# Seven-product blocks issued in program order on four engines, and the weights' sums moved to GpSimd

## The chip, the cores and the metric

The kernel runs on one core of a Trainium2 chip. The engines named here are TensorE (PE; its weight loads are PEld), VectorE (DVE), ScalarE (ACT), GpSimd (POOL) and SyncE (SP), whose queue starts most of the DMA transfers. The metric is the device time of one launch in microseconds, lower is better.

## What is computed

Three layers follow each other on 4 x 768 = 3072 tokens: a retention attention with 8 heads of 64, a gated layer (512 to 1536 and back) behind an RMS norm, and a layer with softmax, layer norm and an output product (512 to 1024 to 512).

```python
state = gamma * state + einsum('bhd,bhe->bhde', k[t], v[t])
y[t]  = scale * einsum('bhd,bhde->bhe', q[t], state)        # attention, one token after the other
xn = x / sqrt(mean(x*x) + 1e-6) * rms_g
g, val = xn @ w_gate, xn @ w_val
x  = (g * sigmoid(g) * val) @ w_out                         # gated layer
h  = x @ w_in
solu = h * softmax(h)
out = (solu - mean) / sqrt(var + 1e-6) * g_ln @ w_out2      # last layer
```

## The kernel before, in words

The tokens run in six blocks of 512 (n = 0 to 5). A block has two parts. In the **gated part** 12 steps (m = 0 to 11) each make 128 columns of gate and 128 of value, and add their share of the output product into four PSUM banks X0 to X3. The **last part** (`de_block`, four tiles of 128 tokens) makes softmax, layer norm and the last product.

Every fp32 product is three fast products: operands are split into a high part (an ACT cast) and a low part (a subtraction), and `mm3` issues high x high, high x low, low x high as three matmuls; in the trace these are L583, L584 and L585 whatever the product.

Blocks 0 and 1 make gate and value with plain products (`bc_block`). Blocks 2 to 5 (`n >= FROM`) use a scheme with seven products for eight (`bc_block7`): a 2 x 2 block product from seven products of sums, `prod(1)` to `prod(7)`, each six matmuls of 256 columns into one of four quarters of the banks GB and VB in turn. So a product waits until the fourth one before it has been taken out of its quarter. One step takes them out so: ACT copies products 1 and 5 (tile `s15`), DVE adds on products 6 and 7 (`u23`), GpSimd adds `u23` and `s15` into `c` twice (L698, L700), and DVE adds products 2, 3 and 4 into `c`. Then ACT makes the Silu of the gate half (L707), DVE multiplies by the value half (L712), and `split` makes the high part (ACT, L89, the tile called r below) and the low part (DVE, L90). `cm(d)` (`cmm`) adds the step **before** into output bank d: three matmuls of 512 columns for each of the four banks.

The seven products need sums of the weights, split as well. The sums are made once, while the last parts of blocks 1 and 0 run one after the other: `s_fetch(m)` loads the weights' parts, `s_make(m)` adds high and low on DVE (L627) into `st` tiles, makes four more sums on GpSimd (L631 to L634) and stores them. In the blocks `s_load(g)` loads a pair of them into two of three `st` buffers, and `s_split(g)` casts both on ACT (L308) and subtracts both on GpSimd (L309).

The attention of block n+1 runs inside the gated part of block n: `att_pieces` gives 24 pieces, three for each of 8 units. Piece a makes scores (PE, an ACT copy, two DVE operations, L151 to L153); piece b makes the other scores, one output product and the next unit's preparation (two ACT casts, two DVE subtractions L117 and L119, two GpSimd products L126); piece c updates the state (GpSimd L191, DVE L194), makes the second output product, the next GpSimd product L135 and, for every second unit, takes out the output with a DVE reduction (L214). `slot(n, s)` calls what is due at slot s, three slots to a step; the 24 pieces fall two to a step. The norm of block n+1 (`rms_steps`) has slots in the last part.

The order of instructions on each engine is not the order in which they are written: when the kernel is built, a scheduler with a model of time arranges all that is ready. Each engine then runs its own row strictly in order, with semaphore waits between the rows.

Of the kernel before, what the change touches and what calls it, by code (L numbers as in the profile page):

```python
# [2 lines left out]

# [6 lines left out]
F32 = mybir.dt.float32  # L10
F32R = mybir.dt.float32r
# [4 lines left out]
ALU = mybir.AluOpType  # L16
AX = mybir.AxisListType

P = 128
# [3 lines left out]
NM = 12  # L23
# [13 lines left out]
FROM = 2  # L37
# [3 lines left out]
def retention_moe_kernel(ctx: ExitStack, tc: tile.TileContext, qk0, q2, kt, kv, wpk, w2i, w2o,  # L41
                         rg, gl, sel, mtab, qtab, ktab, utab, out):
    nc = tc.nc
# [26 lines left out]
    U0 = cp.tile([P, 3, 4, P], F32, tag="w2oh", name="U0")  # L70
    UF = [None, U0[:, 0], U0[:, 1], U0[:, 2], U[0]]

    cnt = [0]

    def wt(tag, shape, dt, bufs):
        cnt[0] += 1
        return wp.tile(shape, dt, tag=tag, name=f"{tag}_{cnt[0]}", bufs=bufs)

    def st():
        return wt("st", [P, 512], F32, 3)  # L80

    def f4():
        return wt("f4", [P, 2, 512], F32, 3)
# [221 lines left out]
    Lq, Hq = slice(0, 256), slice(256, 512)  # L305
# [250 lines left out]
    def at(s, f, *a):  # L556
        wsched.setdefault(s, []).append((f, a))

    def w_plan():
        for g in range(2, NG):  # L560
            for part in range(3):
                if g < NM:
                    s = 3 * (g - 2) + part
                    at(s, w_split, g, part)
                    at(s - 1, w_conv, g, part)
                    at(s - 3, w_load, g, part)
                else:
                    at(3 * g - 4 + part if part < 2 else 3 * g, w_load, g, part)
# [44 lines left out]
    sscr = [[dp.tile([P, 2, 256], F32, tag=f"s{m}_{i}", name=f"s{m}_{i}") for i in range(2)] for m in range(NM)]  # L613
    sums = {}

    def s_fetch(m):
        for part in range(2):
            w = wt("wo", [P, 2, 2, 256], F32R, 2)
            nc.sync.dma_start(w.bitcast(F32), scr[m][part])
            sums[m, part] = w  # L620

    def s_make(m):
        ts = []
        for part in range(2):
            hi, lo = parts(sums.pop((m, part)), part)
            t = st().rearrange("p (h x) -> p h x", h=2)
            nc.vector.tensor_tensor(out=t, in0=hi.bitcast(F32), in1=lo.bitcast(F32), op=ALU.add)  # L627
            ts.append(t)
        g, v = ts
        G = nc.gpsimd  # L630
        G.tensor_tensor(out=v[:, 1], in0=v[:, 0], in1=v[:, 1], op=ALU.add)  # L631
# [3 lines left out]
        for i in range(2):  # L635
            nc.sync.dma_start(sscr[m][i], ts[i])
# [31 lines left out]
    def bc_block7(n):  # L668

        base = 3 * NM * n  # L670
        V, G = nc.vector, nc.gpsimd
        for m in range(NM):
            g = n * NM + m
            c = f4()
            s15, u23 = (wt("r2", [P, 2, 256], F32, 8) for _ in range(2))

            def prod(i):
                q = quarter[0] % 4
                quarter[0] += 1
                ps = GV[q // 2][:, q % 2 * 256:q % 2 * 256 + 256]  # L680
                product(i, g, ps)
                return ps

            def cm(*ds):
                if m:
                    cmm(g - 1, m - 1, ds)

            def add(eng, out, x, y):
                eng.tensor_tensor(out=out, in0=x, in1=y, op=ALU.add)  # L689

            if m + 2 < NM:
                s_load(g + 2)
            nc.scalar.copy(s15[:, 0], prod(1))
            w_slot(base + 3 * m)
            add(V, u23[:, 0], prod(6), s15[:, 0])
            slot(n, 3 * m)
            nc.scalar.copy(s15[:, 1], prod(5))  # L697
            add(G, c[:, 0, Hq], u23[:, 0], s15[:, 1])  # L698
            add(V, u23[:, 1], prod(7), u23[:, 0])
            add(G, c[:, 1, Hq], u23[:, 1], s15[:, 1])  # L700
            cm(0)
            slot(n, 3 * m + 1)
            w_slot(base + 3 * m + 1)
            add(V, c[:, 0, Lq], prod(2), s15[:, 0])
            cm(1)
            add(V, c[:, 0, Hq], prod(3), c[:, 0, Hq])
            nc.scalar.activation(c[:, 0, :], c[:, 0, :], AF.Silu)  # L707
            if m == NM - 1 and n and PRE & 2:
                nc.scalar.activation(wt("sm", [P, 12], F32, 4)[:, 0:1], c[:, 0, 0:1], AF.Exp)
            cm(2)  # L710
            add(V, c[:, 1, Lq], prod(4), u23[:, 1])
            V.tensor_tensor(out=c[:, 1, :], in0=c[:, 1, :], in1=c[:, 0, :], op=ALU.mult)  # L712
            ah, al = r2(), r2()
            split(ah, al, c[:, 1, :])
            acts[m] = (ah, al)
            shl.pop(g)
            if m + 2 < NM:
                s_split(g + 2)
            slot(n, 3 * m + 2 if m < NM - 1 else 34)
            cm(3)  # L720
            w_slot(base + 3 * m + 2)
        cmm(n * NM + NM - 1, NM - 1)

    extra = {}
# [142 lines left out]
    def de_block(n, srcs, base):  # L867

        x2_split(srcs)
        slot(n, base)  # L870
        d_mm(n, 0, base + 1)
        d_mm(n, 1, base + 3)
        t_tr(0)
        d_mm(n, 2, base + 5)
        t_tr(1)
        e_mm(n, 0, base + 7)
        d_mm(n, 3, base + 9)
        t_tr(2)
        e_mm(n, 1, base + 11)
        t_tr(3)  # L880
        e_mm(n, 2, base + 13)
        e_mm(n, 3, base + 15)
# [123 lines left out]
    for n in range(NB):  # L1006
        if n + 1 < NB:
            if n == 0:
                span, r = 30, (31, 33, 34, 34, 35, 35)
            elif n == 1:  # L1010
                span, r = 45, (47, 49, 50, 51, 52, 53, 54, 55, 56, 57)
            else:
                span, r = 35, (37, 38, 39, 40, 41, 42, 43, 44, 45, 46)
            pieces = att_pieces(n + 1)
            for i, f in enumerate(pieces):
                extra.setdefault((n, i * span // (len(pieces) - 1)), []).append(f)
            for s, f in zip(r, rms_steps(SB, n + 1)):
                extra.setdefault((n, s), []).append(f)
        if n + 1 >= FROM and n + 1 < NB:
            for i in range(2):  # L1020
                s, g = (63 if n == 1 else 45) + 3 * i, (n + 1) * NM + i
                extra.setdefault((n, s), []).append(lambda g=g: s_load(g))
                extra.setdefault((n, s + 1), []).append(lambda g=g: s_split(g))
        if n == 1:
            for m in range(NM):
                extra.setdefault((n, 36 + 2 * m), []).append(lambda m=m: s_fetch(m))
                extra.setdefault((n, 37 + 2 * m), []).append(lambda m=m: s_make(m))
        (bc_block if n < FROM else bc_block7)(n)
        if n == 0:
            after.close()  # L1030
            x2_store()
            slot(0, 35)
            continue
        de_block(n, XB, 35)
        if n == 1:
            de_block(0, x2_load(), 52)

# [70 lines left out]
```

## Time and profile before

| | |
|---|---|
| median of 3 runs | 1217.53 us (1216.37 to 1218.59) |
| profiled execution | 1215.62 us, of this span 1213.8 us |
| PE busy | 1062.0 us, 87% of the span |
| DVE, ACT, POOL busy | 736.9, 500.7 and 607.8 us (61%, 41% and 50%) |
| mean granted TensorE clock | 0.960 of full speed |

The profile is one execution. A row of the time line gives the start, the time taken, the engine, the line, what is written from what is read, and in brackets the idle time before it and who ended it. A mean over the span mixes the six blocks, so the stretches are read one by one.

### The profile page before, as it was taken

How to read it: one execution, taken by the hardware profiler on the slowest of the kernel's cores; microseconds unless marked ns; L12 is line 12 of the kernel's file. 1: busy time of each engine (PE TensorE's matmuls, PEld its weight loads, DVE VectorE, ACT ScalarE, POOL GpSimd, SP SyncE). 2: the span in 40 equal slices, each digit the busy share in tenths (PEclk: the TensorE clock that was granted, in tenths of full speed). 3: DMA queues.
4: the chain of work that ended last, by engine and by line, in shares of the span. 5: the costliest groups of instructions: out<-in, count | busy, mean ns of one | idle time of the engine just before them, and what ended most of it. 6: DMA issues, size and time to landing. Idle time of an engine off the chain costs nothing.

```text
span 1213.8 us, 17407 instructions
## 1 busy us (share of the span) xinstructions
PE 1062.0 (87%) x6038; PEld 869.9 (72%) x6038; DVE 736.9 (61%) x1294; ACT 500.7 (41%) x985; POOL 607.8 (50%) x670
## 2 busy tenths in 40 slices
PE   8999999889988698878899878889978889888898
PEld 7777677567766587667688667767767768777777
DVE  6887779972758848753665764464754455334352
ACT  4556655542433454222454322346422245322233
POOL 6866748840567747534254644435444425334222
PEclk9899999989999799899999989989989989999999
DMA  9799888745675736455314555512435521355300
GB/s 335 229 315 348 291 307 288 284 157 187 224 234 183 228 111 210 157 174 182 113 48 146 173 160 179 175 51 83 153 125 195 169 102 53 122 182 183 122 1 35
DMA packets 81239, 212.77 MB, mean 175 GB/s; under 512 B 9472, under 2 KB 9856, under 8 KB 81152
## 3 DMA queue, kind: packets, MB, share of 16 engines
q1 hardware_dynamic: 72368, 186.49, 47.6%
q10 hardware_dynamic: 8784, 25.17, 5.2%
q8 instruction: 48, 0.79, 0.3%
q14 instruction: 39, 0.32, 0.1%
HBM read 179.12 MB, written 32.51 MB: 174 GB/s over the span
## 4 chain that ended last, share of the span: by engine, by line
PE 50%; DVE 17%; issue 8%; ACT 7%; DMA 4%; POOL 3%; DVEq 0%; SPq 0%; POOLq 0%; ACTq 0%
PE X L583 9%; PE X L584 8%; PE X L585 8%; PE GB L583 4%; DVE f L712 4%; PE GB L585 4%; PE GB L584 4%; PE VB L583 4%; PE VB L584 3%; PE VB L585 3%; DMA s<-st 2%; ACT r L89 2%; DVE st L488 2%; ACT x L308 2%; DVE xT L312 1%
## 5 line engine op out<-in xcount | busy, mean ns | idle before, releaser
L309 POOL TENSOR_TENSOR x<-st,x 128x512 fp32r<-128x512 f32 x96 | 133.0, 1404 | 66.2 <-ACT x L308 31.6
L689 POOL TENSOR_TENSOR f<-r,r 128x256 f32<-128x256 f32 x96 | 70.9, 758 | 185.8 <-ACT r L697 96.8
L583 PE MATMUL X<-r,wo 128*128 128x512 f32 x264 | 88.4, 442 | 64.6 <-ACT r L89 64.6
L584 PE MATMUL X<-r,wo 128*128 128x512 f32 x264 | 110.3, 418 | 4.1 <-DVE r L90 4.1
L585 PE MATMUL X<-r,wo 128*128 128x512 f32 x264 | 108.9, 413 | 0.0
L583 PEld LDWEIGHTS X<-r,wo 128*128 128x128 f32 x264 | 48.8, 202 | 81.0 <-ACT r L89 72.6
L308 ACT CAST x<-st 128x512 fp32r<-128x512 f32 x96 | 55.2, 619 | 105.9 <-issue 54.8
L487 POOL TENSOR_TENSOR st<-st,x 128x512 int32<-128x512 int32 x52 | 73.9, 1422 | 42.3 <-DVE st L486 21.9
L126 POOL TENSOR_TENSOR qd<-rq,qtab_t 64x256 f32<-64x256 f32 x68 | 63.9, 939 | 51.9 <-PE YB L163 44.8
L90 DVE TENSOR_TENSOR r<-f,r 128x512 fp32r<-128x512 f32 x72 | 65.9, 915 | 27.6 <-ACT r L89 27.4
L488 DVE SCALAR_TENSOR_TENSOR st<-st,sq 128x512 f32<-128x512 f32 x52 | 62.7, 1205 | 24.1 <-POOL st L487 23.1
L89 ACT CAST r<-f 128x512 fp32r<-128x512 f32 x72 | 44.5, 617 | 75.1 <-DVE f L712 57.5
L712 DVE TENSOR_TENSOR f<-f 128x512 f32<-128x512 f32 x48 | 52.1, 1085 | 21.9 <-ACT f L707 19.1
L584 PEld LDWEIGHTS X<-r,wo 128*128 128x128 f32 x264 | 53.3, 202 | 16.8 <-DVE r L90 6.4
L585 PE MATMUL X<-w2oh,r 128*128 128x512 f32 (+1 forms) x144 | 57.0, 396 | 4.4 <-DVE r L90 4.4
L583 PE MATMUL GB<-xnh,w 128*128 128x256 f32 (+1 forms) x172 | 59.2, 344 | 1.7 <-DVE r L689 1.7
L585 PEld LDWEIGHTS X<-r,wo 128*128 128x128 f32 x264 | 53.2, 202 | 10.5
L583 PE MATMUL VB<-xnh,w 128*128 128x256 f32 (+1 forms) x172 | 58.6, 340 | 0.0
L151 ACT COPY A<-SB 128x256 f32<-128x256 f32 x64 | 23.7, 371 | 83.4 <-PE SB L147 75.5
L583 PE MATMUL X<-w2oh,r 128*128 128x512 f32 (+1 forms) x144 | 57.7, 401 | 0.0
L585 PE MATMUL GB<-xnh,w 128*128 128x256 f32 (+1 forms) x172 | 57.0, 331 | 0.8 <-DVE w L90 0.8
L584 PE MATMUL GB<-xnl,w 128*128 128x256 f32 (+1 forms) x172 | 56.8, 330 | 0.6 <-DVE xnl L280 0.6
(297 smaller groups left out, 3333.2 us busy)
## 6 DMA issues: line engine op xcount, KB each, us to landing
wo<-scr SPq DMA_DIRECT2D x84, 512.0 KB, 3.4
w<-scr SPq DMA_DIRECT2D x72, 512.0 KB, 4.3
st<-s SPq DMA_DIRECT2D x96, 256.0 KB, 3.2
x<-in_wpk SPq DMA_DIRECT2D x36, 512.0 KB, 5.8
w<-scr SPq DMA_DIRECT2D x48, 256.0 KB, 3.3
rq<-in_q SPq DMA_DIRECT2D x40, 256.0 KB, 3.5
rv<-in_kv SPq DMA_DIRECT2D x40, 256.0 KB, 3.9
scr<-CV ACTq DMA_DIRECT2D x18, 512.0 KB, 4.7
```

The lines of the kernel that those rows point to most:

```text
L89: nc.scalar.copy(hi, src)
L90: (lo_eng or nc.vector).tensor_tensor(out=lo, in0=src, in1=hi.bitcast(F32), op=ALU.subtract)
L126: nc.gpsimd.tensor_tensor(out=qd[r], in0=tq4[r, :, hh, :], in1=qtab_t[r, 2 * u:2 * u + 2, :], op=ALU.mult)
L308: nc.scalar.copy(hi, src)
L309: eng.tensor_tensor(out=lo, in0=src, in1=hi.bitcast(F32), op=ALU.subtract)
L487: nc.gpsimd.tensor_tensor(out=ti, in0=ti, in1=lo, op=ALU.add)
L488: lastc[0] = nc.vector.scalar_tensor_tensor(out=t, in0=t, scalar=3.4028234663852886e38, in1=g, op0=ALU.min, op1=ALU.mult)
L583: nc.tensor.matmul(ps, lhsT=lh, rhs=rh, start=start, stop=False)
L584: nc.tensor.matmul(ps, lhsT=lh, rhs=rl, start=False, stop=False)
L585: nc.tensor.matmul(ps, lhsT=ll, rhs=rh, start=False, stop=stop)
L689: eng.tensor_tensor(out=out, in0=x, in1=y, op=ALU.add)
L712: V.tensor_tensor(out=c[:, 1, :], in0=c[:, 1, :], in1=c[:, 0, :], op=ALU.mult)
```

## The change

Around `bc_block7` a context `in_order` chains all instructions that the block issues on PE, DVE, ACT and POOL: each gets an edge, without a semaphore, to the one written before it on its engine. The rows of these four engines are then as written; SP's is not chained. The last instruction of each engine is kept in `tails`, and all of `de_block` is placed behind it. The body of the step is written in another order: `s_split` is for the next step and stands at the step's start, `cm(0)` and `cm(1)` follow products 2 and 3, and `cm(2, 3)` follows the split. `s_make` adds high and low on GpSimd in the load buffers, `s_fetch` runs two steps ahead with the buffers `w4` and `wo`, and the three first weight loads of block 2 (`late`) wait until the sums are done.

```diff
+    @contextmanager
+    def in_order():
+        cur = nc.cur_bb.bb.instructions
+        mark = cur[-1]
+        yield
...
+        for i in cur[start:]:
+            if i.engine in ORDERED:
+                if i.engine in last:
+                    tc.add_manual_dep(i, last[i.engine].name,
...
+                last[i.engine] = i
+        tails.clear()
+        tails.extend(last.values())
+    ORDERED = (E.PE, E.DVE, E.Activation, E.Pool)
...
     def s_fetch(m):
-        for part in range(2):
-            w = wt("wo", [P, 2, 2, 256], F32R, 2)
+        for part, (tag, bufs) in enumerate((("w4", 3), ("wo", 2))):
+            w = wt(tag, [P, 2, 2, 256], F32R, bufs)
...
     def s_make(m):
-            t = st().rearrange("p (h x) -> p h x", h=2)
-            nc.vector.tensor_tensor(out=t, in0=hi.bitcast(F32), in1=lo.bitcast(F32), op=ALU.add)
-            ts.append(t)
...
+        for hi, lo in (g, v):
+            G.tensor_tensor(out=hi.bitcast(F32), in0=hi.bitcast(F32), in1=lo.bitcast(F32), op=ALU.add)
...
+            nc.scalar.copy(s15[:, 0], prod(1))
+            add(V, u23[:, 0], prod(6), s15[:, 0])
+            if m + 1 < NM:
+                s_split(g + 1)
             if m + 2 < NM:
                 s_load(g + 2)
-            nc.scalar.copy(s15[:, 0], prod(1))
             w_slot(base + 3 * m)
-            add(V, u23[:, 0], prod(6), s15[:, 0])
             slot(n, 3 * m)
             nc.scalar.copy(s15[:, 1], prod(5))
             add(G, c[:, 0, Hq], u23[:, 0], s15[:, 1])
             add(V, u23[:, 1], prod(7), u23[:, 0])
             add(G, c[:, 1, Hq], u23[:, 1], s15[:, 1])
-            cm(0)
+            add(V, c[:, 0, Lq], prod(2), s15[:, 0])
             slot(n, 3 * m + 1)
             w_slot(base + 3 * m + 1)
-            add(V, c[:, 0, Lq], prod(2), s15[:, 0])
-            cm(1)
+            cm(0)
             add(V, c[:, 0, Hq], prod(3), c[:, 0, Hq])
             nc.scalar.activation(c[:, 0, :], c[:, 0, :], AF.Silu)
-            cm(2)
+            cm(1)
             add(V, c[:, 1, Lq], prod(4), u23[:, 1])
             V.tensor_tensor(out=c[:, 1, :], in0=c[:, 1, :], in1=c[:, 0, :], op=ALU.mult)
             split(ah, al, c[:, 1, :])
-            if m + 2 < NM:
-                s_split(g + 2)
             slot(n, 3 * m + 2 if m < NM - 1 else 34)
-            cm(3)
+            cm(2, 3)
             w_slot(base + 3 * m + 2)
...
-        (bc_block if n < FROM else bc_block7)(n)
+            with in_order():
+                bc_block7(n)
...
-        de_block(n, XB, 35)
+            for i in tails:
+                later.enter_context(tc.issue_after(i))
+            de_block(n, XB, 35)
```

On PE, in a step of block 5 before, the output product of a step (tile r, banks X_68 to X_71) stands as four high x high matmuls right behind the products (GB and VB are the banks of the quarters):

```order
L584 MATMUL VB<-xsl,x_1332_9257 128x256
L585 MATMUL VB<-xsh,x_1333_9258 128x256
L583 MATMUL X_68<-r_1342_9341,wo_9282 128x512
L583 MATMUL X_69<-r_1342_9341,wo_9282 128x512
L583 MATMUL X_70<-r_1342_9341,wo_9282 128x512
L583 MATMUL X_71<-r_1342_9341,wo_9282 128x512
L583 MATMUL GB<-xsh,x_1332_9257 128x256
```

After the change it stands, in the same block, bank by bank between products 2, 3 and 4:

```order
L612 MATMUL GB<-xnh,w_1368_9676 128x256
L610 MATMUL X_68<-r_1378_9754,wo_9705 128x512
L611 MATMUL X_68<-r_1379_9755,wo_9705 128x512
L612 MATMUL X_68<-r_1378_9754,wo_9705 128x512
L610 MATMUL GB<-xnh,x_1372_9695 128x256
```

So the output product now comes five products after the step that feeds it, and its first bank alone is behind product 2.

On ACT, the row of one step of block 5 before is: both copies (L693, L697), the two casts of the sums, the Silu and the cast of r:

```order
L693 COPY r_1396_9709<-GB 128x256
L697 COPY r_1396_9709<-VB 128x256
L308 CAST x_1404_9785<-st_9711 128x512
L308 CAST x_1404_9785<-st_9713 128x512
L707 ACTIVATE f_1395_9708<-f_1395_9708 128x512
L89 CAST r_1402_9781<-f_1395_9708 128x512
```

After the change the casts stand between the two copies:

```order
L716 COPY r_1394_9855<-VB 128x256
L329 CAST x_1396_9871<-st_9789 128x512
L329 CAST x_1396_9871<-st_9791 128x512
L724 COPY r_1394_9855<-GB 128x256
L733 ACTIVATE f_1393_9854<-f_1393_9854 128x512
L110 CAST r_1402_9930<-f_1393_9854 128x512
L716 COPY r_1406_9943<-VB 128x256
```

The first copy of the next step is now directly behind the cast of r in every step.

On GpSimd, a stretch of block 2 before has the attention (qd, kd, U), the sums' subtractions (x) and the two adds into c (tile f) in mixed order:

```order
L126 TENSOR_TENSOR qd_5044<-rq_4939,qtab_t 64x256 x2
L135 TENSOR_TENSOR kd_4937<-rv_4747,ktab_t 128x256
L191 TENSOR_TENSOR U_82<-U_81,utab_t 64x2x64 x2
L309 TENSOR_TENSOR x_616_4079<-st_3969,x_615_4078 128x512
L309 TENSOR_TENSOR x_616_4079<-st_3971,x_615_4078 128x512
L126 TENSOR_TENSOR qd_5621<-rq_5147,qtab_t 64x256 x2
L135 TENSOR_TENSOR kd_5145<-rv_4943,ktab_t 128x256
L191 TENSOR_TENSOR U_82<-U_81,utab_t 64x2x64 x2
L689 TENSOR_TENSOR f_618_4089<-r_620_4091,r_619_4090 128x256 x2
```

After the change a step with pieces b and c reads:

```order
L330 TENSOR_TENSOR x_630_4302<-st_4194,x_629_4301 128x512
L330 TENSOR_TENSOR x_630_4302<-st_4196,x_629_4301 128x512
L147 TENSOR_TENSOR qd_4330<-rq_4215,qtab_t 64x256 x2
L714 TENSOR_TENSOR f_626_4284<-r_628_4286,r_627_4285 128x256 x2
L212 TENSOR_TENSOR U_81<-U_82,utab_t 64x2x64 x2
L156 TENSOR_TENSOR kd_4371<-rv_4219,ktab_t 128x256
```

Both subtractions and the piece at the step's first slot now stand ahead of the adds into c; the attention is spread two pieces to a step over the whole block, where before it ran ahead.

## Rows read from the trace of the kernel before

**Rows 1.** Windows: PE, PEld, DVE, ACT, POOL busy (count), PEclk, DMA share, GB/s
```profile
446.20:597.87 151.67, 125.39 (x825) 106.52 (x824) 96.72 (x167) 58.56 (x121) 79.27 (x79) 0.94 0.54 171
648.50:799.04 150.54, 121.47 (x797) 103.47 (x795) 94.28 (x158) 55.50 (x114) 74.49 (x78) 0.93 0.52 168
850.00:990.43 140.43, 115.20 (x739) 99.90 (x739) 76.52 (x131) 48.81 (x99) 59.45 (x55) 0.95 0.48 156
1037.00:1161.95 124.95, 103.08 (x655) 91.37 (x655) 49.51 (x86) 36.10 (x73) 44.76 (x45) 0.99 0.45 146
597.87:648.50 50.63, 50.63 (x244) 40.74 (x244) 25.82 (x67) 22.96 (x48) 19.54 (x31) 1.00 0.20 61
307.30:446.20 138.90, 115.86 (x557) 90.89 (x556) 96.87 (x198) 55.71 (x117) 90.18 (x121) 0.91 0.63 199
```

**Rows 2.** Time line of PE: first of six, first of eight, the next product
```profile
744.18 0.28 PE L583 MATMUL GB<-xsh,x 128*128 128x256 f32 x1
...
744.88 0.39 PE L584 MATMUL X<-r,wo 128*128 128x512 f32 x1
...
746.71 0.28 PE L583 MATMUL VB<-xnh,x 128*128 128x256 f32 x1
```

**Rows 3.** Time line of PE in block 5: two output products, two steps apart
```profile
1078.14 1.21 PE L583 MATMUL X<-r,wo 128*128 128x512 f32 x4 [1.45 <-ACT r L89]
...
1098.36 1.19 PE L583 MATMUL X<-r,wo 128*128 128x512 f32 x4 [1.48 <-ACT r L89]
```

**Rows 4.** Groups by line and shape, ACT, 649 to 799 us: busy, mean ns, idle
```profile
L707 ACT ACTIVATE f<-f 128x512 f32<-128x512 f32 x12 | 7.5, 628 | 4.1 <-DVE f L689 4.1
L89 ACT CAST r<-f 128x512 fp32r<-128x512 f32 x12 | 7.4, 618 | 13.3 <-DVE f L712 13.3
L151 ACT COPY A<-SB 128x256 f32<-128x256 f32 x13 | 4.8, 370 | 22.3 <-PE SB L147 22.2
```

**Rows 5.** The same view for POOL, 649 to 799 us
```profile
L309 POOL TENSOR_TENSOR x<-st,x 128x512 fp32r<-128x512 f32 x20 | 27.7, 1400 | 9.3 <-PE GB L585 3.3 <-PE VB L585 3.3 <-ACT x L308 2.3
L689 POOL TENSOR_TENSOR f<-r,r 128x256 f32<-128x256 f32 x24 | 17.7, 756 | 37.5 <-ACT r L697 24.6 <-DVE r L689 12.8
L126 POOL TENSOR_TENSOR qd<-rq,qtab_t 64x256 f32<-64x256 f32 x10 | 9.2, 922 | 11.0 <-PE YB L163 10.6
L191 POOL TENSOR_TENSOR U<-U,utab_t 64x128 f32<-64x128 f32 x12 | 6.0, 499 | 1.9 <-DVE U L194 1.5
L135 POOL TENSOR_TENSOR kd<-rv,ktab_t 128x256 f32<-128x256 f32 x7 | 5.8, 835 | 3.7 <-issue 2.1 <-PE SB L178 1.4
```

**Rows 6.** The same view for DVE, 649 to 799 us
```profile
L712 DVE TENSOR_TENSOR f<-f 128x512 f32<-128x512 f32 x12 | 13.4, 1117 | 4.4 <-ACT f L707 3.7
L153 DVE TENSOR_TENSOR A<-A,mtab_t 128x256 f32<-128x256 f32 x13 | 9.1, 699 | 0.3
L117 DVE TENSOR_TENSOR kst<-rk,kst 64x512 fp32r<-64x512 f32 x7 | 7.4, 1055 | 0.2
L689 DVE TENSOR_TENSOR f<-GB,r 128x256 f32<-128x256 f32 x12 | 5.1, 425 | 10.4 <-PE GB L585 10.4
L214 DVE TENSOR_REDUCE ssq<-sq 128x128 f32<-128x512 f32 x3 | 3.2, 1058 | 0.3 <-ACT sq L213 0.3
L312 DVE SCALAR_TENSOR_TENSOR xT<-xT,rg_t,ssq 128x512 f32<-128x512 f32 x4 | 4.0, 1062 | 0.0
```

**Rows 7.** Time line of block 5: a GpSimd pair, and two DVE operations of one size
```profile
1094.59 2.52 POOL L309 TENSOR_TENSOR x<-st,x 128x512 fp32r<-128x512 f32 x2 [0.23 <-ACT x L308]
...
1096.00 1.66 DVE L712 TENSOR_TENSOR f<-f 128x512 f32<-128x512 f32 x1
...
1098.34 0.69 DVE L90 TENSOR_TENSOR r<-f,r 128x512 fp32r<-128x512 f32 x1 [0.69 <-ACT r L89]
```

**Rows 8.** DMA issues: KB each, median us from issue to landing
```profile
st<-s SPq DMA_DIRECT2D x96, 256.0 KB, 3.2
```

**Rows 9.** Groups by line and shape, DVE, 307 to 446 us
```profile
L627 DVE TENSOR_TENSOR st<-wo 128x512 f32<-128x512 f32 x24 | 18.1, 754 | 15.4 <-DMA s<-st 10.2 <-DMA wo<-scr 2.9 <-POOL sm L814 1.6
```

More of the change, by code (lines that the diff above doesn't have):

```diff
@@ L1 @@
 from collections import deque
-from contextlib import ExitStack, nullcontext
+from contextlib import ExitStack, contextmanager, nullcontext
 import concourse.bass as bass
@@ L71, in retention_moe_kernel @@
     UF = [None, U0[:, 0], U0[:, 1], U0[:, 2], U[0]]
+    @contextmanager
[3 more added lines that the diff above has]
+        yield
+        last = {}
+        start = next(k for k in reversed(range(len(cur))) if cur[k] is mark) + 1
+        for i in cur[start:]:
+            if i.engine in ORDERED:
+                if i.engine in last:
+                    tc.add_manual_dep(i, last[i.engine].name,
+                                      mybir.DependencyInfo(mybir.DependencyClass.NoSync, mybir.DependencyReason.DATA),
+                                      reason="in_order")
+                last[i.engine] = i
+        tails.clear()
+        tails.extend(last.values())
+    tails = []
+    E = mybir.EngineType
+    ORDERED = (E.PE, E.DVE, E.Activation, E.Pool)
     cnt = [0]
@@ L557, in at @@
         wsched.setdefault(s, []).append((f, a))
+    late = []
     def w_plan():
@@ L567, in w_plan @@
                 else:
-                    at(3 * g - 4 + part if part < 2 else 3 * g, w_load, g, part)
+                    s = 3 * g - 4 + part if part < 2 else 3 * g
+                    if part < 2 and s < 3 * FROM * NM <= 3 * g:
+                        late.append((g, part))
+                    else:
+                        at(s, w_load, g, part)
         w2 = [("in", i) for i in range(8)] + [("out", i) for i in range(8)]
@@ L622, in s_make @@
     def s_make(m):
-        ts = []
-        for part in range(2):
-            hi, lo = parts(sums.pop((m, part)), part)
-            t = st().rearrange("p (h x) -> p h x", h=2)
-            nc.vector.tensor_tensor(out=t, in0=hi.bitcast(F32), in1=lo.bitcast(F32), op=ALU.add)
-            ts.append(t)
-        g, v = ts
+        g, v = (parts(sums.pop((m, part)), part) for part in range(2))
         G = nc.gpsimd
+        for hi, lo in (g, v):
+            G.tensor_tensor(out=hi.bitcast(F32), in0=hi.bitcast(F32), in1=lo.bitcast(F32), op=ALU.add)
+        g, v = g[0].bitcast(F32), v[0].bitcast(F32)
         G.tensor_tensor(out=v[:, 1], in0=v[:, 0], in1=v[:, 1], op=ALU.add)
@@ L634, in s_make @@
         G.tensor_tensor(out=g[:, 1], in0=g[:, 1], in1=g[:, 0], op=ALU.subtract)
-        for i in range(2):
-            nc.sync.dma_start(sscr[m][i], ts[i])
+        nc.sync.dma_start(sscr[m][0], g)
+        nc.sync.dma_start(sscr[m][1], v)
     sf, shl = {}, {}
@@ L1019, in retention_moe_kernel @@
         if n + 1 >= FROM and n + 1 < NB:
[L1020 to L1023, printed above, removed]
+            s, g = 63 if n == 1 else 45, (n + 1) * NM
+            extra.setdefault((n, s), []).append(lambda g=g: s_load(g))
+            extra.setdefault((n, s + 2), []).append(lambda g=g: (s_split(g), s_load(g + 1)))
         if n == 1:
+            extra.setdefault((n, 35), []).append(lambda: (s_fetch(0), s_fetch(1)))
             for m in range(NM):
-                extra.setdefault((n, 36 + 2 * m), []).append(lambda m=m: s_fetch(m))
-                extra.setdefault((n, 37 + 2 * m), []).append(lambda m=m: s_make(m))
-        (bc_block if n < FROM else bc_block7)(n)
+                extra.setdefault((n, 37 + 2 * m), []).append(
+                    lambda m=m: (s_make(m), s_fetch(m + 2) if m + 2 < NM else None))
+            extra.setdefault((n, 61), []).append(lambda: [w_load(*x) for x in late])
+        if n < FROM:
+            bc_block(n)
+        else:
+            with in_order():
+                bc_block7(n)
         if n == 0:
@@ L1033, in retention_moe_kernel @@
             continue
-        de_block(n, XB, 35)
+        with ExitStack() as later:
+            for i in tails:
+                later.enter_context(tc.issue_after(i))
+            de_block(n, XB, 35)
         if n == 1:
```

## Prediction

> **What bounds the kernel now.** I first cut the span into its stretches, with the busy time of each engine in each. The four gated parts with seven products take 151.7, 150.5, 140.4 and 125.0 us, 567.6 together. In them PE is idle for a sixth to a fifth of the time (block 5: 103.1 busy of 125.0), and in blocks 2 to 4 the granted clock falls to 0.93 to 0.95 of full speed. The last part behind block 2 is PE busy from end to end (50.63 of 50.63), so there is nothing to win in it [rows 1]. No engine is full in the gated parts: in block 3 DVE is busy 94.3 of 150.5, POOL 74.5, ACT 55.5. So they are bound by waits, not by work.
>
> What must PE do there? The time line at full clock shows six matmuls of a product in 0.70 us (744.18 to 744.88) and eight of the output product in 1.83, so three in 0.69 [rows 2]. A step is seven products and four times three: 7 x 0.70 + 4 x 0.69 = 7.66 us, twelve are 91.9. Block 5, which has no attention, needs 10.1 us for a step (1078.14 to 1098.36 for two), and each time PE stands 1.5 us before the output product, waiting for ACT's cast L89 [rows 3]. Blocks 2 to 4 have the attention as well: by PE's busy time some 12.1 us more (115.2 in block 4 against 103.1) [rows 1].
>
> **The output product moves back five products.** From the end of product 4 the chain is DVE add 0.43, multiplication 0.69 to 1.12, ACT cast 0.62: about 2 us [rows 4, 6, 7]. In its new place the output product starts two banks and five products later, 1.4 + 3.5 = 4.9 us. So the wait of 1.5 us goes. What is late next? In program order a step has a loop of its own that PE does not show. The first ACT copy of a step stands behind the cast of r of the step before; behind the copy stand the casts of the sums; on GpSimd both subtractions stand ahead of the add into c; the add frees DVE's add on product 3, then Silu, multiplication and the cast of r. In a step without attention: copy 0.37, cast 0.62, two subtractions 2.80, GpSimd add 0.76, DVE add 0.43, Silu 0.63, multiplication 0.69, cast 0.62 = 6.92 us [rows 4 to 7]. That is below PE's 7.66, with 0.7 to spare for the hand-overs, so block 5 runs at PE's pace: 91.9, and I add 6 for its filling and draining (the first step has no output product behind it, the last one must wait for its own cast). 98 against 125.0: **27 us less**.
>
> The loads are no new bound by this: a pair of sums lands 3.2 us after its issue [rows 8], and is issued when a subtraction frees its buffer, four to five us ahead of its cast in the next step.
>
> **Blocks 2 to 4: the loop with attention in it.** The pieces come two to a step, in a pattern of three steps: (a,b), (c,a), (b,c). I walk the loop through each.
>
> (a,b): b's GpSimd products stand behind the adds, so DVE leads. Copy 0.37, u23 0.43, scores of a (0.43 + 0.70), u23 0.43, product 2 0.43, scores of b 1.13, the two preparations 2 x 1.06, product 3 0.43, Silu 0.63, multiplication at its mean 1.12, cast 0.62: 8.84 us [rows 4, 6, 7].
>
> (c,a): GpSimd leads; the state's two products and kd (2 x 0.50 + 0.84) stand ahead of the adds: 6.92 + 1.84 + 0.43 for the dearer multiplication = 9.19 us [rows 5, 6].
>
> (b,c): copy and cast 0.99, subtractions 2.80, two products of the preparation 1.84, both adds 1.52, the state's two products 1.00; then DVE adds to the state (at most the 0.43 of a larger add) and reduces the attention's output 1.06, and only then takes product 3 out: 0.43 + 0.63 + 1.12 + 0.62. Together 12.44 us [rows 4 to 6]. What is queued behind the waiting add on DVE are products 3 and 4, and PE's third and fourth product from there wait for these quarters.
>
> The three make 30.5 us, four times that is 122; hand-overs and the ends of the block I put at 4 more, an estimate: 126 us. PE alone would need 91.9 + 12.1, so PE waits 20 us in such a block, less than now. Three blocks: 442.6 - 378 = **64.6 us less**.
>
> **The last parts.** All of `de_block` now stands behind the block, and the norm of the next block with it: at its four places it puts operations like L312 at 1.06 us on DVE, 4.2 us in all [rows 6], between those of the layer norm, while PE has no idle time that could cover them [rows 1]. From nothing (DVE is busy 25.8 of 50.6 there) to 4.2 a block; I take 2, **6 us more** for three blocks.
>
> **The sums.** 24 additions of 128 x 512 leave DVE, 18.1 us [rows 9]. On GpSimd the nearest row is a subtraction of the same size at 1.40 [rows 5]: 33.6 us. In the stretch of 138.9 us GpSimd goes from 90.2 busy to 124, and the layer norm's own GpSimd operations stand between the sums. PE is idle there for 23 us [rows 1], and DVE, which waited 10.2 us for the sums' stores [rows 9], gets room. From 6 less (a third of DVE's 18.1) to 25 more (the added work without its share of the idle time); I take **5 more**, nearer to no change because GpSimd still has 15 us free.
>
> **The sum.** 64.6 + 27.0 - 6 - 5 = 80.6 less than the profiled execution's 1215.6: 1135.0 us. The median of the runs is 1.9 above that execution, so 1137.
>
> [...] Rows first: the multiplication took 1.66 us while a pair of GpSimd subtractions ran, and an operation of its size with GpSimd idle 0.69 [rows 7]; its mean in block 3 is 1.12 [rows 6]. [...]
>
> **The rivals.**
> - *PE's pace everywhere.* If the loops overlap better than walked (parts of DVE's and ACT's rows run ahead while GpSimd works), blocks 2 to 4 take 91.9 + 12.1 + 6 = 110 us: 112.6 + 27 less, and nothing lost in the last parts and the sums: 1217.5 - 139.6 = 1078. For it: no engine has more work than PE's 104 us (DVE 94.3 in block 3 with the norm). Against: (b,c), where the operations wait for each other across three engines.
> - *Last parts and sums at their upper bounds*, 12.6 and 25 instead of 6 and 5: 1164. For it: a last part has no PE idle time to give.
> - *Attention blocks keep their time.* If every step with attention costs the 12.4 of (b,c), a block takes 150 as now; only block 5 gains: 1217.5 - 27 + 11 = 1202.
> - *Slower: GpSimd and DVE block each other.* In a step of blocks 2 to 4 four DVE operations with two SBUF inputs stand in the chain: one of the scores, two preparations, the multiplication. If each waits for a whole GpSimd operation of 1.40, that is 5.6 us, of which the means used already hold about 1.5 (1.12 and 1.06 against 0.69, 0.70 against 0.43) [rows 5 to 7]. Then a step costs 10.5 + 4.1 = 14.6, three blocks 526, 83 more than now; with 19 less in block 5 and 11 for the rest, 1217.5 + 75 = 1293. It decides from a step of 12.7 us on, where the three blocks lose what block 5 wins (442.6 + 27 - 11 over 36). Against: the two subtractions stand early in the step, the multiplication late.
> - *The edges order nothing that mattered*, the time stays: against it stand the rows of the three engines, which are moved.
>
> **Chances.** Forecast with its own range of 1105 to 1165: 0.53. PE's pace 0.15. Upper bounds of the last parts and the sums 0.12. Attention blocks keep their time 0.08. No change 0.03. Slower 0.09. A run of this kernel tells 0.2%, 2.4 us, from no change: faster 0.88, same 0.03, slower 0.09. The range from 1080 to 1190 holds the forecast, the upper bounds and about half of the two cases that touch its ends, 0.77 to 0.8.
>
> **What would show it.** In block 5 the output product follows a product with no wait for L89, two steps take about 15.5 us instead of 20.2, and the granted clock is full. In block 3 a stretch of three steps takes 30 us and one of them 12, and PE's waits there are for DVE's adds on products 3 and 4 and for the copies, not for the cast of r. GpSimd is busy about 124 us while the sums are made, in a stretch of some 144 us, and a last part takes 52 to 53. The prediction is wrong if the three-step pattern is not there, by PE being at its pace (rival one) or by DVE's operations with two SBUF inputs at 2 us each (the slower rival).

## The result, and the profile after

The changed kernel takes 1172.32 us (median of 3 runs, 1170.69 to 1180.65) against 1217.53 before; the ratio is 0.9647, with a 95% interval of 0.9575 to 0.9719. It is 45 us faster where I had forecast 80: the sign is right, the time is inside the wide range of 1080 to 1190, but outside the 1105 to 1165 that I gave the forecast itself. In the ratios of the experiments below, runs over 1.5% longer than the fastest of their kernel, with a lower granted clock, are left out.

The profiled execution is the longest of the three, 1180.65 us, span 1178.9. It lost 12 us before the change begins: its first product of the last part stands at 320.2 us against 308.3 before. Nearly all of that (11 us) lies in the first 65 us, in which PE was busy but the granted clock was 0.71 of full speed; the kernel before did the same work in 54 us at 0.94. The columns are those of [rows 1], the first row is from the kernel before, the other two are from the changed kernel:

```profile
0.00:54.00 54.00, 48.99 (x380) 40.47 (x381) 38.21 (x60) 27.68 (x52) 41.52 (x49) 0.94 0.81 277
0.00:65.00 65.00, 61.70 (x379) 49.29 (x380) 36.81 (x60) 27.03 (x52) 40.77 (x49) 0.71 0.65 228
65.00:319.30 254.30, 236.14 (x1136) 177.17 (x1135) 189.83 (x247) 134.06 (x233) 150.46 (x129) 0.99 0.80 276
```

From there on the two executions can be compared. The windows of the changed kernel (gated parts of blocks 2 to 5, the last part behind block 2, the stretch of the sums):

```profile
439.50:579.22 139.72, 120.32 (x815) 100.95 (x813) 81.63 (x151) 55.64 (x111) 65.06 (x78) 0.96 0.61 185
630.90:767.09 136.19, 117.96 (x812) 99.14 (x810) 81.95 (x150) 56.12 (x112) 60.71 (x70) 0.99 0.61 191
818.80:959.03 140.23, 121.87 (x819) 103.22 (x818) 80.39 (x148) 54.99 (x110) 63.56 (x75) 0.96 0.57 177
1013.35:1127.01 113.66, 99.62 (x642) 85.72 (x642) 43.30 (x86) 37.73 (x73) 42.09 (x44) 1.00 0.51 162
579.22:630.90 51.68, 49.98 (x236) 40.51 (x235) 33.61 (x75) 25.22 (x52) 26.80 (x34) 1.00 0.15 47
319.30:439.50 120.20, 108.46 (x499) 85.85 (x497) 71.83 (x150) 49.42 (x102) 103.58 (x127) 0.94 0.61 204
```

These gated parts begin at the end of the last product of the last part before them. By that border, which is somewhat later than the one in [rows 1], the kernel before has 151.0, 149.7, 136.3 and 121.3 us, with the last parts behind blocks 2 to 4 at 51.5, 55.1 and 50.3, and the two last parts with the sums at 138.6. I use this border from here on:

| us | before | changed | forecast |
|---|---|---|---|
| two last parts with the sums | 138.6 | 119.3 | 5 more |
| gated parts, blocks 2, 3, 4 | 151.0, 149.7, 136.3 | 139.7, 136.2, 140.2 | 126 each |
| gated part, block 5 | 121.3 | 113.7 | 98 |
| last parts, blocks 2, 3, 4 | 51.5, 55.1, 50.3 | 51.7, 51.7, 54.3 | 2 more each |

So the gated parts won 28.5 us, not 92, the last parts lost 0.8, and the sums, where I had put a loss, won 19.3. With the 12 us of the start these make the 35 us between the two spans. The rows of the table do not hold the same work: before, attention ran ahead into the stretch of the sums, and the chain ends that. The stretch has 499 matmuls for 557, PE busy 108.5 us for 115.9; block 4 has 818 for 739, and is 3.9 us longer.

The wait of [rows 3] before the output product is gone in block 5, as forecast; only the last output product, which adds the step just done, still waits 0.6 us for its cast. What has come in its place is seen on PE in a step of block 5. This is its time line around two pairs of products (1 and 6 in bank VB, 5 and 7 in GB); rows inside a product are left out:

```profile
1067.43 0.28 PE L612 MATMUL VB<-xnh,w 128*128 128x256 f32 x1
1068.18 0.39 PE L610 MATMUL VB<-xsh,x 128*128 128x256 f32 x1 [0.46 <-ACT r L716]
...
1068.98 0.28 PE L610 MATMUL GB<-xnh,x 128*128 128x256 f32 x1
...
1069.55 0.28 PE L612 MATMUL GB<-xnh,x 128*128 128x256 f32 x1
1070.29 0.38 PE L610 MATMUL GB<-xsh,x 128*128 128x256 f32 x1 [0.46 <-ACT r L724]
```

And ACT's two copies in the same place:

```profile
1067.75 0.37 ACT L716 COPY r<-VB 128x256 f32<-128x256 f32 x1 [0.16 <-PE VB L612]
...
1069.86 0.37 ACT L724 COPY r<-GB 128x256 f32<-128x256 f32 x1 [0.70 <-PE GB L612]
```

Product 6 begins 0.75 us after the last matmul of product 1, where 0.12 is the pace; it begins 0.06 us after ACT's copy of product 1 is done (1067.75 + 0.37), although that copy reads the other quarter of the bank. Product 5, in the other bank, begins at PE's pace behind product 6 (whose last matmul starts at 1068.87, the next at 1068.98). The same between 5 and 7. Two steps take 18.7 us (copies L716 at 1058.25, 1067.75 and 1076.92) instead of 20.2, where I had forecast 15.5. Over block 5 I added up, along the time line, what each start comes later than the pace of [rows 2], where that is over 0.25 us: 18.5 us, of which 17.2, at 25 places, stand before a product whose neighbour ahead is in the same bank. Of the other signs that I had named, the granted clock of block 5 is full; three steps of block 3 take 34.8 us from 641.0 on where I had 30; and GpSimd is busy 103.6 us while the sums are made, not 124.

### The profile page after: what moved, and what is told of

It is laid out like the page before. It is cut to its first block, busy times and chain, and to the rows that moved or that the text cites. A ratio compares the mean times of both kernels' runs of the same rounds, so it can differ in the third digit from the quotient of the medians.

```text
span 1178.9 us, 17166 instructions
## 1 busy us (share of the span) xinstructions
PE 1065.9 (90%) x6038; PEld 864.5 (73%) x6038; DVE 708.6 (60%) x1270; ACT 508.9 (43%) x985; POOL 619.2 (53%) x694
## 4 chain that ended last, share of the span: by engine, by line
PE 51%; DVE 14%; POOL 8%; issue 6%; ACT 4%; DMA 2%; ACTq 0%; DVEq 0%; POOLq 0%; SPq 0%
PE X L611 7%; PE X L610 7%; PE X L612 7%; PE GB L610 6%; PE VB L610 5%; PE GB L612 4%; PE GB L611 4%; PE VB L612 4%; PE VB L611 4%; POOL x L330 2%; DVE st L509 2%; DVE r L714 1%; DVE qhl L140 1%; DVE kst L138 1%; PE X L827 1%
## 5 line engine op out<-in xcount | busy, mean ns | idle before, releaser
L330 POOL TENSOR_TENSOR x<-st,x 128x512 fp32r<-128x512 f32 x96 | 123.6, 1307 | 219.7 <-ACT x L329 204.7
L610 PE MATMUL X<-r,wo 128*128 128x512 f32 x264 | 105.2, 415 | 5.5 <-ACT r L110 5.5
L611 PE MATMUL X<-r,wo 128*128 128x512 f32 x264 | 106.3, 403 | 3.6 <-DVE r L111 3.6
L612 PE MATMUL X<-r,wo 128*128 128x512 f32 x264 | 105.3, 399 | 0.0
L733 ACT ACTIVATE f<-f 128x512 f32<-128x512 f32 x48 | 30.3, 632 | 122.2 <-DVE f L714 122.2
L111 DVE TENSOR_TENSOR r<-f,r 128x512 fp32r<-128x512 f32 x72 | 55.9, 777 | 38.0 <-ACT r L110 37.9
L610 PE MATMUL VB<-xnh,w 128*128 128x256 f32 (+1 forms) x172 | 59.8, 348 | 19.3 <-DVE r L714 13.7
L147 POOL TENSOR_TENSOR qd<-rq,qtab_t 64x256 f32<-64x256 f32 x68 | 61.1, 899 | 20.2 <-PE YB L184 17.6
L610 PEld LDWEIGHTS X<-r,wo 128*128 128x128 f32 x264 | 50.2, 193 | 16.5 <-ACT r L110 7.8
L611 PEld LDWEIGHTS X<-r,wo 128*128 128x128 f32 x264 | 50.9, 193 | 11.5 <-DVE r L111 6.2
L612 PEld LDWEIGHTS X<-r,wo 128*128 128x128 f32 x264 | 50.8, 192 | 11.1
L610 PE MATMUL X<-w2oh,r 128*128 128x512 f32 (+1 forms) x144 | 56.9, 395 | 0.2 <-ACT r L110 0.2
L612 PE MATMUL VB<-xnh,w 128*128 128x256 f32 (+1 forms) x172 | 57.1, 332 | 0.0
L611 PE MATMUL VB<-xnl,w 128*128 128x256 f32 (+1 forms) x172 | 57.0, 331 | 0.0
```

Source lines behind the costliest of these rows:

```text
L111: (lo_eng or nc.vector).tensor_tensor(out=lo, in0=src, in1=hi.bitcast(F32), op=ALU.subtract)
L147: nc.gpsimd.tensor_tensor(out=qd[r], in0=tq4[r, :, hh, :], in1=qtab_t[r, 2 * u:2 * u + 2, :], op=ALU.mult)
L330: eng.tensor_tensor(out=lo, in0=src, in1=hi.bitcast(F32), op=ALU.subtract)
L610: nc.tensor.matmul(ps, lhsT=lh, rhs=rh, start=start, stop=False)
L611: nc.tensor.matmul(ps, lhsT=lh, rhs=rl, start=False, stop=False)
L612: nc.tensor.matmul(ps, lhsT=ll, rhs=rh, start=False, stop=stop)
```

## The experiments

All times are medians; each ratio is to runs of the kernel before on the same chip.

**Banks in turn.** My theory after the result: a product waits until the other quarter of its bank is taken out. The rival: the loop through ACT, GpSimd and DVE that I had walked sets the step.

```diff
-                ps = GV[q // 2][:, q % 2 * 256:q % 2 * 256 + 256]
+                ps = GV[q % 2][:, q // 2 * 256:q // 2 * 256 + 256]
```

> One expression differs from the changed kernel: successive products go to the two banks in turn, where the changed kernel fills both quarters of one bank one after the other. Theory one (a product waits until the other quarter of its bank has been taken out, whoever reads it): in block 5 of the changed kernel 17.2 us of PE's gaps stand before a product that follows one in its own bank, in block 3 16.7 us; with another product between, 0.7 us, nearly all of it is covered: block 5 from 113.7 to 96 to 99 us, blocks 2 to 4 12 to 16 us shorter each, the whole 1172 to 1110 to 1125. Rival (the loop through ACT, GpSimd and DVE sets the step, and the bank only shows where PE happens to stand): block 5 stays within 3 us of 113.7 and the whole within 1% of 1172, with the same idle time before other products.

Measured: 1104.28 us, ratio 0.9086 (0.9062 to 0.9109). Windows of the gated parts, columns as above:

```profile
427.80:550.08 122.28, 113.60 (x813) 97.24 (x812) 80.89 (x151) 54.55 (x111) 68.55 (x78) 1.00 0.65 212
602.70:722.37 119.67, 112.49 (x804) 97.11 (x803) 80.59 (x149) 55.09 (x112) 63.37 (x70) 1.00 0.67 218
775.16:899.78 124.62, 114.93 (x812) 98.83 (x811) 79.26 (x147) 53.62 (x110) 66.67 (x75) 1.00 0.62 197
954.69:1049.81 95.12, 93.47 (x638) 85.70 (x637) 43.17 (x86) 37.61 (x73) 42.16 (x44) 1.00 0.60 192
```

They are 17.4, 16.5, 15.6 and 18.6 us shorter than in the changed kernel, and the granted clock is full in all four. In block 5 of the changed kernel PE's waits for the copies and adds are 13.2 us in the view of waits, 25 of them; its two largest groups:

```profile
PE GB L610 <- DVE r L714: 3.6, 6, 0.9
PE VB L610 <- DVE r L714: 3.3, 6, 0.6
...
```

With the banks in turn one wait of 0.8 is left of them:

```profile
PE VB L610 <- ACT r L716: 0.8, 1, 0.8
PE X L610 <- ACT r L110: 0.6, 1, 0.6
```

A step of block 5 takes 7.8 us (999.71 - 991.93 between the first copies), PE's own pace, which I had put at 7.66:

```profile
991.93 0.37 ACT L716 COPY r<-VB 128x256 f32<-128x256 f32 x1 [0.16 <-PE VB L612]
...
999.71 0.37 ACT L716 COPY r<-GB 128x256 f32<-128x256 f32 x1 [0.16 <-PE GB L612]
```

The theory holds, the rival falls for block 5. The gain of 68 us is somewhat above the 47 to 62 expected. This version beats both kernels.

It was run once more beside two later kernels:

> The kernel with the banks in turn once more, on the chip of the two others: 1100 to 1108.

1103.24 us, ratio 0.9058 (0.9006 to 0.9110).

**The scheduler's order with the rest of the change.**

```diff
-            with in_order():
-                bc_block7(n)
+            bc_block7(n)
```

> The changed kernel without the chain: the scheduler orders the four engines in the gated parts again; the rewritten step, the sums on GpSimd and the late loads stay. If the gated parts win by the written order, blocks 2, 3 and 5 go back to 151, 150 and 121 us and the whole stands near 1172 + 29 = 1200. Rival (the sums alone make the gain; the order gives nothing): the whole stays at 1165 to 1180.

1199.51 us, ratio 0.9890 (0.9832 to 0.9949). Gated parts 150.4, 142.6, 136.1 and 121.3. The first theory holds for blocks 2 and 5, not for block 3, which keeps 7 us of its gain. The chain is worth 27 us. What is left, 16 to 18 us against the kernel before, is that of the rest of the change: in the profiles the stretch of the sums is 14 us shorter (124.2), block 3 is 7 shorter, and the last parts behind blocks 2 to 4 are 3 longer.

**Banks in turn in the kernel before.** The same expression as above, nothing else.

> The kernel before with the one expression on the banks changed: successive products in the two banks in turn. In block 5 of the kernel before only 4.1 us of PE's gaps stand before a product in the bank of the one before it, against 20.6 before the output product, so if the same-bank wait is the written order's own cost, the whole gains 0 to 15 us, against 67 in the changed kernel. Rival (the bank is worth the same in any order): 1150 to 1165.

1161.51 us, ratio 0.9581 (0.9519 to 0.9643), 53 us less: the rival's time came, if not quite its 68 us. The gated parts become 140.3, 133.2, 119.8 and 109.3, 11 to 17 us shorter each. The gaps before products of the same bank (4.1 us in block 5) had not shown it. In block 5 of the kernel before, PE's row takes the products out of the written order so that neighbours are in one bank only once in two steps. With the banks in turn the scheduler arranges another row: no same-bank neighbours are left, PE starts the output product mostly 1.2 us later than its pace instead of 1.5 to 1.9, and a step takes 9.2 us instead of 10.1.

**Banks in turn without the chain.** Both edits above together.

> The kernel with the banks in turn, without the chain: the scheduler orders the gated parts. With it the four corners are there: pairs and free order 1199.5, pairs and written order 1172, turns and written order 1104. If order and banks are worth the same whatever the other is (27 and 68), this one takes 1199.5 - 68 = 1132. If the order is worth more once the banks no longer stop it, it takes 1138 to 1155, as the kernel before with the banks in turn (1161.5) less the 16 to 20 of the sums. Rival (the order is worth nothing with the banks in turn): 1100 to 1110.

1154.13 us, ratio 0.9488 (0.9412 to 0.9565). The second of the three came, at its upper end: banks in turn are worth 45 us in this kernel in the scheduler's order and 68 in the written one; the written order is worth 27 with pairs and 50 with turns. In block 5 what is left in the scheduler's order is the wait of [rows 3] again:

```profile
PE X L610 <- ACT r L110: 12.8, 12, 2.5
```

**The sums: three kernels.** First the addition of high and low back on DVE, in the load buffers.

```diff
-            G.tensor_tensor(out=hi.bitcast(F32), in0=hi.bitcast(F32), in1=lo.bitcast(F32), op=ALU.add)
+            nc.vector.tensor_tensor(out=hi.bitcast(F32), in0=hi.bitcast(F32), in1=lo.bitcast(F32), op=ALU.add)
```

> The changed kernel with the addition of high and low back on DVE, in the load buffers; fetching two ahead with five buffers stays. The stretch of the sums took 139.6 us before and 120.2 after. If the gain there is DVE's 18 us of additions, the stretch goes back to 135 to 140 and the whole is 15 to 20 us slower than the changed kernel. Rival (the gain is the earlier fetch with more buffers, which ends the waits for loads and stores): the stretch stays at 115 to 123, the whole within 5 us of the changed kernel, or a little below it, since GpSimd is busy 103.6 of 120 there.

1171.17 us, ratio 0.9633 (0.9605 to 0.9662); the stretch takes 117.9. Which engine adds makes no difference that shows.

Then the sums into `st` tiles on DVE as before, fetched two steps ahead:

```diff
...
+            t = st().rearrange("p (h x) -> p h x", h=2)
+            nc.vector.tensor_tensor(out=t, in0=hi.bitcast(F32), in1=lo.bitcast(F32), op=ALU.add)
+            ts.append(t)
...
+            nc.sync.dma_start(sscr[m][i], ts[i])
```

> The changed kernel with the sums made as before, on DVE into st tiles, but fetched two steps ahead with five buffers. If adding in the load buffers made the gain, the stretch goes back to 133 to 142 us and the whole to 1185 to 1195; if the fetch made it, the stretch stays below 125.

1170.62 us, ratio 0.9619 (0.9597 to 0.9642); the stretch takes 122.9. Adding in the load buffers is not the gain either.

Last, the additions on GpSimd in the load buffers, but fetched as before:

```diff
-        for part, (tag, bufs) in enumerate((("w4", 3), ("wo", 2))):
+        for part, (tag, bufs) in enumerate((("wo", 2), ("wo", 2))):
...
-            extra.setdefault((n, 35), []).append(lambda: (s_fetch(0), s_fetch(1)))
...
+                extra.setdefault((n, 36 + 2 * m), []).append(lambda m=m: s_fetch(m))
...
```

> The changed kernel with the weights for the sums fetched as before, one step ahead into two buffers; the additions stay on GpSimd in these buffers. If the earlier fetch with five buffers made the stretch of the sums 20 us shorter, it goes back to 133 to 142 us and the whole to 1185 to 1195. Rival (adding in the load buffers did it, since no sum waits for a store of the three st tiles): the stretch stays below 125, the whole below 1178.

1204.81 us, ratio 0.9912 (0.9879 to 0.9946), 32 more than the changed kernel, but not where I expected it. The last parts take 109.2 us; then block 2's gated part takes 183.7, because PE waits for output weights whose buffers the sums still hold:

```profile
PE X L610 <- DMA wo<-scr: 42.8, 1, 42.8
```

With the last parts and block 2's gated part together: 289.6 before, 259.0 changed, 257.4 and 262.3 with the sums on DVE, 292.9 with the old fetch. So sums in their load buffers need the five buffers and the earlier fetch: such a sum holds its buffer until its store is done, and with the old two buffers it is no better than before. How much of the gain the fetch makes where the sums go to `st` tiles is not shown: these with the old fetch in the written order were not run, nor was the change without its late loads.

**The last part not placed behind the gated part.**

```diff
-            for i in tails:
-                later.enter_context(tc.issue_after(i))
```

> The changed kernel without the edge that puts the last part behind the gated part; the chain in the gated part stays. My prediction put 2 us for each of three last parts on the norm of the next block, which this edge keeps out of the gated part. If that is so, the last parts behind blocks 2 to 4 (51.7, 51.7 and 54.3 us) become 2 to 4 us shorter each and the whole 5 to 10 us faster. Rival (without the edge instructions of the last part get between those of the gated part and are in the way of the chain): the gated parts become longer, the whole 0 to 20 us slower.

1171.60 us, ratio 0.9635 (0.9616 to 0.9655). Last parts 53.3, 54.0 and 55.7, gated parts within 3 us: no effect on the whole that shows, so neither theory. Here the edge costs the whole nothing and gives it nothing.

**The attention's pieces called later.** In the kernel with the banks in turn:

```diff
-            slot(n, 3 * m)
             nc.scalar.copy(s15[:, 1], prod(5))
...
             add(G, c[:, 1, Hq], u23[:, 1], s15[:, 1])
+            slot(n, 3 * m)
             add(V, c[:, 0, Lq], prod(2), s15[:, 0])
-            slot(n, 3 * m + 1)
...
             shl.pop(g)
+            slot(n, 3 * m + 1)
```

> The kernel with the banks in turn, and in its step the attention's pieces called later: the first behind GpSimd's adds into c, the second behind the split of r. In the kernel with the banks in turn a step with pieces b and c takes 12.2 us, with a and b 10.1, with c and a 9.3, near the loop I walked (12.4, 8.8, 9.2), in which GpSimd's work for the attention stands ahead of the adds and DVE's ahead of product 3. If that loop sets these steps, taking the attention out of it leaves PE's pace: 8.7 to 9.5 us a step, blocks 2 to 4 from 122, 120 and 125 to 108 to 114 us each, the whole from 1104 to 1070 to 1085. Rival (these steps are set by the engines' work or by the pieces' own waits, wherever the pieces stand): the blocks stay at 118 to 125, the whole at 1095 to 1110, or slower where pieces now wait for each other.

1123.22 us, of four runs from 1111.25 to 1131.25; the ratio, 0.9150 (0.9116 to 0.9183), is that of 1111.25 and 1115.35. Gated parts 129.2 (at a granted clock of 0.97), and at full clock 124.6, 124.9 and 94.5: not shorter. The rival holds. (The expectation has the two shorter steps the wrong way round: by the instructions in them, 9.4 us is a step with a and b, 10.1 one with c and a.)

Only the second piece moved (the last two of these four places):

> The kernel with the banks in turn, and only the second of a step's two pieces moved, behind the split of r. In it a step with b and c took 12.2 us, with one stop of about 0.9 us for DVE's add on product 3, which stands behind c's updates and reduction. If c on DVE sets this stop, blocks 2 to 4 become 3 to 8 us shorter each and the whole 1082 to 1096. Rival (moving both pieces gave nothing, and the blocks are near PE's work of 109 us, 91.9 for the steps and 17 for the attention): the whole stays within 1% of 1104, or is slower.

1108.16 us, ratio 0.9100 (0.9047 to 0.9152), against 1103.24 for the kernel with the banks in turn on the same chip. Gated parts 125.9, 122.5, 123.6 and 95.1. The rival again. The stop for DVE's add on product 3 is gone (in block 3, 2.2 us in the view of waits before, none now) and the step with b and c is shorter by 0.5 us (11.7 for 12.2), but PE waits instead for DVE's adds into `u23`, and the blocks are not shorter:

```profile
PE VB L610 <- DVE r L714: 3.2, 3, 1.1
PE GB L610 <- DVE r L714: 2.9, 4, 1.3
```

## Why the prediction came out as it did

**The wait that was to go.** Right: in block 5 the 1.5 us before the output product are gone in every step, and the chain alone is worth 27 us (1199.5 to 1172).

**Block 5: 98 us forecast, 113.7 measured.** The step that failed is the rule under the whole walk, that a product waits only for the fourth one before it, whose quarter it takes. It waits as well for its neighbour in the same bank: product 6 began 0.75 us behind the last matmul of product 1, where 0.12 is the pace. Written in order, products 1 and 6, 5 and 7, 2 and 3 follow each other in one bank, or with the other parity 6 and 5, 7 and 2, 3 and 4. Where part of the output product stands between two of them, as between 2 and 3, it covers the wait (one product 3 of block 5 begins at 1072.47, 0.24 us after the start of the matmul of 512 columns before it, at PE's pace); in block 5 PE stops twice a step, 25 times in all, for a copy or an add that I had counted as covered. It cost 18.6 us in block 5 and 15.6 to 17.4 in each of the others, 68 in all. By the sum of late starts used above, over all four parts, PE's stops fall from 89 to 34 us, which is 55 of the 68; the other 13 are, by an estimate from the granted clocks of 0.96, 0.99 and 0.96 over blocks 2 to 4, what the clock's lower level (0.50, as from 496.0 to 502.5 us in block 2) cost. With the same-bank wait taken away block 5 takes 95.1 us, and its step 7.8. In the trace PE waits for the reader of the other quarter: of the 25 waits in block 5 of the changed kernel 11 are for ACT's copies (5.1 us), 12 for DVE's adds into `u23` (6.9 us) and 2 for DVE's adds into `c`. A run without these waits and with the same banks was not made.

**Blocks 2 to 4: 126 us each forecast, 136 to 140 measured, 120 to 125 without the same-bank waits.** The size was near once the missing term is gone, and a pattern of three steps is there (12.2, 9.4 and 10.1 us for (b,c), (a,b) and (c,a) in block 4 with the banks in turn; I had 12.4, 8.8 and 9.2). But the cause that I gave is not borne out, and the near size is luck: two kernels take attention out of the loop, which shortens the long step by half a microsecond (to 11.6 and 11.7) and no block. PE's windows in block 3 with the banks in turn say why, for a step with pieces b and c and the two behind it (PE busy, granted clock, DMA share, GB/s):

```profile
621.50:633.70 12.20, 11.24 (x82) 1.00 0.74 227
633.70:643.00 9.30, 9.00 (x63) 1.00 0.46 158
643.00:651.20 8.20, 8.20 (x60) 1.00 0.87 312
```

PE itself is busy 28.4 of 29.7 us. I had put the attention on PE at 12.1 us a block, from the difference in busy time of blocks 4 and 5 before. But block 4 held only part of its attention there, since the rest had run ahead: it had 84 matmuls more than block 5 (739 and 655 [rows 1]), and has 176 more in the changed kernel (818 and 642). With the banks in turn, at full clock, PE is busy 112.5 us in block 3 and 93.5 in block 5, so the attention is 19 and not 12. In the long step PE is idle 1.0 us, most of it in one stop: it begins product 1 of the next step 0.9 us later than its pace, waiting for DVE's add on product 3, which shares its bank. So the loop exists, but is worth about 1 us in one step of three, not the 4 that I gave it.

**The sums: 5 more forecast, 19 less measured.** The sign was wrong. I priced the engines' work, 33.6 us on GpSimd for 18.1 on DVE. That costs nothing that shows, since the kernel with these additions on DVE takes the same. GpSimd is busy 103.6 of 120.2 us in the stretch and not 124 of 144: three of the additions stand ahead of this window, and some 10 us of its attention work are no longer in it.

I left out two things. The first is that attention leaves the stretch: with the scheduler's order and the rest of the change the stretch takes 124.2, so some 5 of the 19 us come from the chain, and block 4 gives 4 back. The second is the other half of the edit, the fetch. Before, DVE stood 10.2 us for the stores of the `st` tiles and 2.9 for loads [rows 9]. After, GpSimd's additions wait for a few us in all:

```profile
L654 POOL TENSOR_TENSOR wo<-wo 128x512 f32<-128x512 f32 x12 | 16.4, 1367 | 5.1 <-DMA wo<-scr 1.9 <-DMA s<-w 1.6 <-PE SB L168 1.5
L654 POOL TENSOR_TENSOR w<-w 128x512 f32<-128x512 f32 x9 | 11.8, 1311 | 1.9 <-DMA w<-scr 1.9
```

The price of an addition was right (1.31 to 1.37 against 1.40). By which way the earlier fetch saves PE's time stays open. That DVE stands less for stores is not it: with the sums in `st` tiles and the earlier fetch DVE still stands 13.3 us for them, and the whole is as fast (1170.62):

```profile
L655 DVE TENSOR_TENSOR st<-wo 128x512 f32<-128x512 f32 x12 | 8.4, 702 | 12.9 <-DMA s<-st 8.7 <-issue 2.4 <-DMA wo<-scr 1.1
L655 DVE TENSOR_TENSOR st<-w 128x512 f32<-128x512 f32 x11 | 8.3, 754 | 4.9 <-DMA s<-st 4.6 <-issue 0.3
```

**The last parts: 6 more forecast, 0.8 measured.** The norm is in them (DVE 33.6 us busy instead of 25.8) and is covered.

**The rivals.** PE's pace in every step did come, in the version with the banks in turn, at 1104 and not at the 1078 that I gave it, mostly since attention costs PE 7 us a block more. The upper bounds of the last parts and the sums (1164) came near in number alone: the sums won time. Attention blocks that keep their time (1202) came for block 4 only. That the edges order nothing is refuted by the 27 us of the chain. The rival of GpSimd and DVE blocking each other did not come: the multiplication took 0.693 us on the mean in block 3, where it had 1.117 before [rows 6], because in the written order it stands where GpSimd is idle: no GpSimd instruction of the trace overlaps any of these twelve. In block 3 before, it took 0.69 in the three places with no GpSimd instruction beside it, and 0.80 to 1.69 in the nine others. A wait for a whole GpSimd operation of 1.40, as this rival supposed, does not show in it: the longest of the 48 multiplications of the kernel before took 1.75, 1.06 more than 0.69.

```profile
L738 DVE TENSOR_TENSOR f<-f 128x512 f32<-128x512 f32 x12 | 8.3, 693 | 2.1 <-ACT f L733 0.8
```

The sum, set right: the gated parts won 28.5 us for 91.6, 63 too little; the sums took 24 us less than I gave them and the last parts 5 less: 1137 + 63 - 24 - 5 = 1171, against 1172 measured. The same-bank waits that I did not have are 68 us; against them stand 14 by which the gated parts without these waits are below my 126 and 98 (461.7 for 476), and the other 9 come from the later border, by which these parts took 558.3 us before and not 567.6. Two large errors of opposite sign are why the time still fell between 1080 and 1190.

## What to carry to other kernels

Before products are written in a fixed order, lay out which of them share a PSUM bank and let neighbours differ in it: here one index expression was worth 68 us in the written order, more than the order itself, and 45 to 53 in the scheduler's order, where no single wait in the profile named it. Where an edit moves work to another engine and also changes how its loads are fetched, price both: the moved work was free, and taking the fetch back cost 32 us. Before PE's share of an interleaved job is taken from the difference of two stretches, count its matmuls in them: a scheduler may have moved half of the job elsewhere.

## What the runs showed of the hardware that was not expected

The granted TensorE clock stood at 0.71 of full speed in the first 65 us of one execution, with PE busy 61.7 of them, where the kernel before shows 0.94 in the same work; the part ahead of the last parts was 12 us longer. The profile of the kernel with both pieces moved shows 0.66 in its first 65 us and has its first product of the last part at 324.0 us, while the other ten profiles of the experiments have it between 308.4 and 309.1. What sets this off was not tried.

With the banks in turn the granted clock is full in all four gated parts, where the changed kernel shows 0.96 to 1.00 and the kernel before 0.93 to 0.99 [rows 1]. PE's longest delay before a matmul in the gated parts, by the sum used above, is 5.0 us before, 2.9 in the changed kernel and 1.7 with the banks in turn; with the longer stops the time at the lower of the clock's two levels is gone (1.00 and 0.50: in windows of half a microsecond block 2 of the changed kernel shows 1.00 up to 496.0 us, 0.50 from there to 502.5 and 1.00 from 503.0 on). That the stops cause it is not shown apart.
